# Which queues carry v, the stores and the first q and k of an attention and MLP-mixer kernel

## The chip, the cores and the metric

The kernel runs on one core of one Trainium2 chip. The metric is the time of one execution on the device in microseconds. The kernel before took 317.55 us (median of three runs, 316.34 to 318.38).

The engines are named as the profile names them: PE is TensorE, DVE is VectorE, ACT is ScalarE, POOL is GpSimd, SP is SyncE. PE, DVE, ACT and POOL compute, each its own stream of instructions in order; SP here only issues transfers. A transfer is issued from the stream of one engine. Those of SP go by the hardware queue q1, those of ACT by the hardware queue q10, those of POOL by the software queue q0. On POOL an issue shows up as an instruction of that engine.

## The reference

The inputs are q, k and v of 8 batches, 8 heads, 576 positions and 64 values per head, 8 indices of global positions, and four weight matrices. Everything is float32.

```python
scores = scale * np.matmul(q, k.transpose(0, 1, 3, 2))
mask = np.abs(pos[:, None] - pos[None, :]) <= 32
mask = mask | is_global[:, None] | is_global[None, :]
scores = np.where(mask, scores, -1000000000.0)
attn = softmax(scores)                       # exp and division by the sum
x = np.matmul(attn, v)                       # (8, 576, 512), heads side by side
h = np.maximum(x.transpose(0, 2, 1) @ w_tok1, 0.0) @ w_tok2
u = x + h.transpose(0, 2, 1)
out = u + np.maximum(u @ w_ch1, 0.0) @ w_ch2
```

It is attention inside a window of 32 positions on either side, with 8 positions that see all and are seen by all, then an MLP over the 576 positions (to 256 and back) and one over the 512 channels (to 1536 and back), each added to its input.

## The kernel before

**Tiling.** The work goes batch by batch, b = 0 to 7. The 576 positions are four tiles of 128 and a last one of 64. q and k come in as float32 into the single buffers `lq` and `lk` (positions 0 to 511, two transfers of four heads each, three smaller ones in batch 0) and `lr` (the last 64 positions of both); v comes into the single buffer `lv`, five transfers, one for each tile. `cast_qk` turns q and k to float16 (`qk`, `rn`), `cast_v` turns v into `vsh`, and `shift_v` copies a half-tile shift of it to `vod`. q and k must be transposed: for batches 0 to 2 (below `PEB` = 3) PE does it (`turn_pe`, `rest_pe`), and for batches 3 to 7 nine DMA transposes of each batch do it from SP (`turn_dma`, lines 639 and 643), after which DVE copies `raw` to `qT` and `kT` (lines 651 and 654).

**Stages of a batch.** `scores` multiplies the window's blocks, ACT takes exp into `e` (line 683), DVE masks (line 689). The rows of the global positions come in by an indirect load on POOL (`f_gather`, line 487) into `g32`, are cast (line 617) and transposed in `glob_rows`; batch 0 has its global rows out of `glob_pe` instead, so the gathered rows serve batches 1 to 7, in two groups. `values` multiplies by v and DVE normalises into `x` (lines 780 to 790). `token1` and `token2` are the MLP over positions; their sum `u` is transposed by `turn_u`, by PE for batches 0 to 2 and by DMA from SP after that (lines 843 and 853). `chan1` multiplies by the first channel weight (line 866), ACT or DVE evict with relu (lines 858 and 860), `chan2` multiplies by the second (line 895) and DVE adds `u` into one of three `osb` buffers (line 903), from which a transfer of 256 KB stores a tile of the output. The last tiles of two batches share one `osb` and go out as two transfers (line 909).

**What sets the order.** Every step is entered with `op`: the engines that may do it with their costs, a priority, what it reads and writes, and for a transfer `dma` = (time on the DMA engines, packet size, latency, packets). `behind` names steps that must have been issued before. Then `run` plans the whole kernel as the program is built. It places step after step on the engine that is free first, by priority among those that could start about then, and models the queues and their sharing of the DMA engines. For a transfer that is planned after 36 us its users are planned another 2 us later, and `late` adds to that for one step. The plan fixes only the order of each engine's stream; on the chip an engine waits until its next instruction can start. So a changed cost or queue can change the order on every engine.

**Who issues what.** SP: q, k and v of batch 0, q and k of batches 3 to 7, all DMA transposes, all stores. ACT: v of batches 3 to 7 (five issues a batch, 25 in all). POOL: the weights, which are cast on the way, the gathers, q and k of batches 1 and 2, v of batches 1 and 2. `gate` makes POOL wait for the first v tiles of batch 0 before it issues the weights and what comes behind them. After the second gather POOL has nothing to do.

Of the kernel before, what the change touches and what calls it, by code (L numbers as in the profile page):

```python
# [15 lines left out]
P = 128  # L16
# [11 lines left out]
def kernel(  # L28
# [12 lines left out]
    nc = tc.nc  # L41
# [845 lines left out]
    def chan2(b, tau, pri):  # L887
# [17 lines left out]
        if not last:  # L905
            op([("S", 0.45)], pri + 5, lambda e: nc.sync.dma_start(out=out[b, P * tau : P * tau + P, :], in_=osb), r=[("osb", o)], dma=STORE)
        else:
            for z in range(2):
                op([("S", 0.45)], pri + 5, lambda e, z=z: nc.sync.dma_start(
                    out=out[b - 1 + z, S - LAST : S, :], in_=osb[64 * z : 64 * z + 64]), r=[("osb", o)], dma=(0.39, 2048, 0.8, 64))  # L910
# [11 lines left out]
    def loads(b, n0=0):  # L922
        pl = 100.0 * b - 145 if b != 1 else -174.0
        if b == 0:
# [6 lines left out]
            return  # L931
        if b < PEB:
            if b == 1:
                pl = -173.9
            load_rest(b, pl, [("G", 0.73)], [n0] if b == 1 else ())
            for h in range(0, H, 4):
                for ti in range(2):
                    load_qk(b, ti, slice(h, h + 4), pl + 1 + h / 2 if b > 1 else pl + 0.1 + h / 100, [("G", 0.88)], [n0] if b == 1 else ())
            if b > 1:
                load_v(b, pl + 6, [("G", 0.87)])  # L940
        else:
            load_rest(b, pl, [("S", 0.65)])
# [13 lines left out]
    for b in range(B):  # L956
# [102 lines left out]
```

## Time and profile before

| | |
|---|---|
| median of the runs | 317.55 us (316.34 to 318.38, three runs) |
| the profiled execution | 317.08 us, of which the span of the records is 315.4 us |
| mean granted clock of PE | 0.984 |
| matrix multiplications of the channel MLP (lines 866 and 895) | 93.3 and 87.8 us of PE's busy time |
| bytes moved by DMA | 51.31 MB, mean 163 GB/s |
| share of the 16 DMA engines' span: q1, q0, q10 | 48.7%, 16.5%, 9.9% |

All times in the profile are from one execution, in microseconds from the start of the span. The engines' busy times overlap. A queue's share is the time of its packets against 16 engines; when several queues run at once the shares can add up to more than 1. In a timeline a line gives the start, the duration, the engine, the line of the kernel, the operation, what it writes and reads, how many such instructions are merged, and in brackets how long the engine had been idle before it and whose end released it. A name with a q at the end, such as SPq or ACTq, is the engine's sequencer, which issues transfers and handles semaphores. A list of waits gives the waiting instruction, what it waited for, then the total in us, how often, and the longest.

### The profile page before, as it was taken

The page shows a single profiled execution, that of the slowest core. Times are in us where ns is not written, and L with a number is a line of the kernel's source. Part 1 is how long each engine was busy: PE and PEld are TensorE (multiplying, and loading weights), DVE is VectorE, ACT ScalarE, POOL GpSimd, SP SyncE. Part 2 cuts the span into 40 slices and gives each one's busy share as a digit, 9 for nine tenths or more (in the row PEclk, how much of TensorE's full clock was granted, in tenths as well). Part 3 has the DMA queues.
Part 4 walks back from the last instruction along what each step waited for, and adds up shares of the span by engine and source line. Part 5 has one row for each costly group of instructions (what it writes and reads, how often), then busy time and mean ns, then how long its engine had stood idle before and what let it go on. Part 6 is the DMA issues. An engine that isn't in the chain of part 4 may idle for free.

```text
span 315.4 us, 7280 instructions
## 1 busy us (share of the span) xinstructions
PE 291.4 (92%) x2944; PEld 153.3 (49%) x2944; DVE 187.6 (59%) x413; ACT 178.7 (57%) x322; POOL 44.5 (14%) x81
## 2 busy tenths in 40 slices
PE   6968989997999898999999996799999999999993
PEld 3635645453474444444475443444465445444641
DVE  7588867569777587586675657772554257230021
ACT  4872895479996484965985693541832182305500
POOL 8588735620000000000000000000000000000000
PEclk9779999999999999799999999999999999999999
DMA  6999999999599979999999989415001401051013
GB/s 179 253 135 295 207 221 246 275 254 265 122 238 214 209 207 301 162 217 223 310 164 153 304 192 203 109 22 164 33 2 31 137 35 36 11 160 49 2 67 100
DMA packets 96452, 51.31 MB, mean 163 GB/s; under 512 B 73698, under 2 KB 89954, under 8 KB 96418
## 3 DMA queue, kind: packets, MB, share of 16 engines
q1 hardware_dynamic: 66512, 33.83, 48.7%
q0 software_dynamic: 6464, 11.11, 16.5%
q10 hardware_dynamic: 23442, 5.90, 9.9%
q8 instruction: 23, 0.38, 0.5%
q14 instruction: 11, 0.09, 0.1%
HBM read 36.11 MB, written 9.44 MB: 144 GB/s over the span
## 4 chain that ended last, share of the span: by engine, by line
PE 49%; DMA 24%; DVE 11%; ACT 10%; issue 2%; SPq 2%; ACTq 1%; POOL 0%; DVEq 0%
PE bank L895 19%; PE bank L866 16%; DMA raw<-qk 9%; DMA lq<-in_q_dram 5%; DMA g_q<-in_q_dram,idx_i 4%; PE bank L821 3%; ACT e L683 3%; PE bank L803 3%; ACT b L858 3%; DMA lk<-in_k_dram 2%; PE bank L673 2%; ACT qk L534 2%; PE bank L878 2%; DVE qT L569 1%; DMA lv<-in_v_dram 1%
## 5 line engine op out<-in xcount | busy, mean ns | idle before, releaser
L866 PE MATMUL bank<-uT,wc 128*128 128x512 f16 x384 | 93.3, 384 | 3.6 <-DVE qT L589 1.3
L895 PE MATMUL bank<-wc,b 128*128 128x512 f16 x384 | 87.8, 379 | 0.1
L858 ACT ACTIVATE b<-bank 128x512 f16<-128x512 f32 x86 | 50.9, 614 | 42.8 <-PE bank L866 36.9
L683 ACT ACTIVATE e<-bank 128x648 f16<-128x648 f32 x64 | 42.8, 730 | 35.0 <-PE bank L673 33.9
L895 PEld LDWEIGHTS <-b 128*128 128x128 f16 x384 | 36.9, 98 | 43.5 <-issue 0.4
L866 PEld LDWEIGHTS <-wc 128*128 128x128 f16 x384 | 35.3, 98 | 45.1 <-issue 6.9
L903 DVE TENSOR_TENSOR osb<-u,bank 128x512 f32<-128x512 f16 x32 | 21.7, 685 | 40.5 <-PE bank L895 40.2
L689 DVE TENSOR_TENSOR e<-e,masku 128x1296 f16<-128x1296 f16 x28 | 23.2, 830 | 17.0 <-ACT e L683 16.7
L546 ACT CAST vsh<-lv 128x512 f16<-128x512 f32 (+3 forms) x44 | 27.1, 620 | 5.2 <-DMA lv<-in_v_dram 4.1
L834 DVE TENSOR_TENSOR u<-x,bank 128x512 f16<-128x512 f16 x30 | 18.7, 682 | 13.1 <-PE bank L821 12.8
L781 DVE TENSOR_TENSOR x<-bank,rr 128x512 f16<-128x512 f32 x32 | 22.1, 691 | 1.1
L740 PE MATMUL bank<-rf,lf 128*64 128x264 f16 x144 | 15.1, 278 | 5.8 <-ACT b L858 2.0
L821 PE MATMUL bank<-a,w 128*128 128x512 f16 x80 | 19.9, 379 | 0.3 <-DVE a L809 0.2
L651 DVE COPY kT<-raw 128x512 f16<-128x512 f16 x20 | 12.0, 601 | 13.5 <-DMA raw<-qk 13.4
L803 PE MATMUL bank<-x,w 128*128 128x512 f16 x64 | 19.2, 387 | 0.5 <-DMA lq<-in_q_dram 0.4
L673 PEld LDWEIGHTS <-kT 64*128 64x128 f16 x576 | 11.6, 98 | 14.7 <-issue 13.9
L534 ACT CAST qk<-lq 128x512 f16<-128x512 f32 x26 | 15.9, 623 | 4.0 <-DMA lq<-in_q_dram 4.0
L534 ACT CAST qk<-lk 128x512 f16<-128x512 f32 x27 | 16.6, 625 | 2.6 <-DMA lk<-in_k_dram 2.6
L673 PE MATMUL bank<-qT,kT 64*128 64x72 f16 x576 | 15.9, 199 | 0.5 <-ACT e L683 0.4
L753 PEld LDWEIGHTS <-e 128*64 128x64 f16 x576 | 15.3, 111 | 0.2
L753 PE MATMUL bank<-vsh,e 128*64 128x66 f16 x320 | 15.3, 194 | 0.0
L654 DVE COPY qT<-raw 128x512 f16<-128x512 f16 x20 | 11.9, 601 | 4.8 <-DMA raw<-qk 4.8
(163 smaller groups left out, 321.2 us busy)
## 6 DMA issues: line engine op xcount, KB each, us to landing
out_dram<-osb SPq DMA_DIRECT2D x32, 256.0 KB, 2.5
lq<-in_q_dram SPq DMA_DIRECT2D x11, 512.0 KB, 6.2
lk<-in_k_dram SPq DMA_DIRECT2D x11, 512.0 KB, 7.6
lv<-in_v_dram ACTq DMA_DIRECT2D x15, 256.0 KB, 5.1
wc<-in_moe_w_ch_dram POOLq DMA_DIRECT2D x6, 512.0 KB, 12.6
lq<-in_q_dram POOLq DMA_DIRECT2D x4, 512.0 KB, 12.1
lk<-in_k_dram POOLq DMA_DIRECT2D x4, 512.0 KB, 10.1
lv<-in_v_dram ACTq DMA_DIRECT2D x10, 192.0 KB, 3.9
```

The source lines that it names most:

```text
L534: COPY[e](out=qk[:, ti, p].rearrange("q i (r d) -> q r i d", r=2), in_=(lq, lk)[ti][:, hs])
L546: COPY[e](out=vsh[i][a:z, c, :, 0:D], in_=lv[a:z, c])
L673: nc.tensor.matmul(ps_tile[keys[z]][:, u // 3, UW * (u % 3) : UW * (u % 3) + UW], lhsT=kT[r, 64 * u : 64 * u + P], rhs=qT[r, u // 2, UW * ...
L683: op([("A", 0.595)], pri + 1, lambda e, par=par: nc.scalar.activation(out=es[i][:, 2 * p + par].rearrange("p (n u) x -> p n u x", n=3), in ...
L689: op([("V", 0.85)], pri + 2, lambda e: nc.vector.tensor_mul(out=e2, in0=e2, in1=masku.unsqueeze(1).to_broadcast([P, 2, NB, UW])), r=["mask ...
L753: nc.tensor.matmul(o[:, VW * hh : VW * hh + VW], lhsT=es[i][:, h, 2 * tau + c, x : x + 64], rhs=vod[i][:, tau, h, :] if c else vsh[i][:, t ...
L781: nc.vector.tensor_tensor(out=xo, in0=pq[:, :, :, 0:D], in1=rr.unsqueeze(3).to_broadcast([P, 2, NP, D]), op=ALU.mult,)
L803: nc.tensor.matmul(ps_tile[key][:, tt], lhsT=w, rhs=x16s[i][:, ch, :], start=(ch == 0), stop=(ch == NT - 1))
L821: nc.tensor.matmul(ps_tile[key], lhsT=w2[:, ch, P * tau - sh : P * tau - sh + P], rhs=a1[:, ch, :], start=(ch == 0), stop=(ch == 1 and not ...
L858: nc.scalar.activation(out=out, in_=in_, func=AF.Relu)
L866: nc.tensor.matmul(ps_tile[key], lhsT=wc1[:, cc, P * j : P * j + P], rhs=uT[:, cc, :], start=(cc == 0), stop=(cc == 3))
L895: nc.tensor.matmul(ps_tile[key], lhsT=w, rhs=wc2[:, j, :], start=(j == 0), stop=(j == NJ - 1))
```

## The change

- **v**: the loads of batches 3 to 7 go from ACT's queue to POOL's. Batch 2 was there already, so v of batches 2 to 7 is on POOL now (30 transfers), planned at 0.87 us each. v of batch 0 stays on SP and of batch 1 on POOL.
- **Stores**: the stores of whole tiles of batches 0 to 6 (28 transfers) go from SP to POOL, planned at 0.8 us each. Batch 7's four stores and the eight of the last tiles stay on SP.
- **q and k**: batches 1 and 2 go from POOL to SP (12 transfers). All q and k is on SP then, planned at 0.55 us an issue instead of 0.5. Those of batch 1 no longer stand behind the gate; they have a priority right after batch 0's v.
- **Order**: the second channel weight's first part is to be issued behind the last part of the first channel weight (`n1`), no longer behind batch 1's loads. The first gather, that of q for the first group, has `late` = 2.3, so the plan has its cast on DVE that much later.

```diff
@@ chan2
         if not last:
-            op([("S", 0.45)], pri + 5, lambda e: nc.sync.dma_start(out=out[b, P * tau : P * tau + P, :], in_=osb), r=[("osb", o)], dma=STORE)
+            op([("G", 0.8) if b < B - 1 else ("S", 0.45)], pri + 5, lambda e: ENG[e].dma_start(out=out[b, P * tau : P * tau + P, :], in_=osb), r=[("osb", o)], dma=STORE)
...
@@ loads
-        if b < PEB:
-            if b == 1:
-                pl = -173.9
-            load_rest(b, pl, [("G", 0.73)], [n0] if b == 1 else ())
-            for h in range(0, H, 4):
-                for ti in range(2):
-                    load_qk(b, ti, slice(h, h + 4), pl + 1 + h / 2 if b > 1 else pl + 0.1 + h / 100, [("G", 0.88)], [n0] if b == 1 else ())
-            if b > 1:
-                load_v(b, pl + 6, [("G", 0.87)])
-        else:
-            load_rest(b, pl, [("S", 0.65)])
-            for h in range(0, H, 4):
-                for ti in range(2):
-                    load_qk(b, ti, slice(h, h + 4), pl + 1 + h / 2, [("S", 0.5)])
-            load_v(b, pl + 6, [("A", 0.6)])
+        load_rest(b, pl, [("S", 0.65)])
+        for h in range(0, H, 4):
+            for ti in range(2):
+                load_qk(b, ti, slice(h, h + 4), pl + 1 + h / 2, [("S", 0.55)])
+        if b > 1:
+            load_v(b, pl + 6, [("G", 0.87)])
@@ the loop over batches
-                op([("G", 2.7)], (-115 if ti == 0 else -174.2) if b == 0 else 70, f_gather(b, ti), r=["idx"], w=[("g32", b, ti)], dma=(0.1, 256, 1.7, 256),
+                op([("G", 2.7)], (-115 if ti == 0 else -174.2) if b == 0 else 70, f_gather(b, ti), r=["idx"], w=[("g32", b, ti)], dma=(0.1, 256, 1.7, 256), late=0.0 if b or ti else 2.3,
...
-            loads(1, n0)
-            op([("G", 0.77)], -40, f_wc2(0), w=[("wc2", 0)], dma=(2.6, 4096, 2.0, 512), behind=[len(ops) - 1])
+            loads(1)
+            op([("G", 0.77)], -40, f_wc2(0), w=[("wc2", 0)], dma=(2.6, 4096, 2.0, 512), behind=[n1])
```

More of the change, by code (lines that the diff above doesn't have):

```diff
@@ L905, in chan2 @@
         if not last:
-            op([("S", 0.45)], pri + 5, lambda e: nc.sync.dma_start(out=out[b, P * tau : P * tau + P, :], in_=osb), r=[("osb", o)], dma=STORE)
+            op([("G", 0.8) if b < B - 1 else ("S", 0.45)], pri + 5, lambda e: ENG[e].dma_start(out=out[b, P * tau : P * tau + P, :], in_=osb), r=[("osb", o)], dma=STORE)
         else:
             for z in range(2):
-                op([("S", 0.45)], pri + 5, lambda e, z=z: nc.sync.dma_start(
+                op([("S", 0.45)], pri + 5, lambda e, z=z: ENG[e].dma_start(
                     out=out[b - 1 + z, S - LAST : S, :], in_=osb[64 * z : 64 * z + 64]), r=[("osb", o)], dma=(0.39, 2048, 0.8, 64))
```

## The prediction

> **What bounds the kernel now.** I read the page's head first, then busy time by stretch, then what TensorE (PE) waited for in each stretch that is not full, and last the engines named there.
>
> ```profile
> span 315.4 us, 7280 instructions
> PE 291.4 (92%) x2944; PEld 153.3 (49%) x2944; DVE 187.6 (59%) x413; ACT 178.7 (57%) x322; POOL 44.5 (14%) x81
> ```
> ```profile
> 0.00:20.00 20.00, 14.21 (x174) 9.73 (x175) 14.75 (x62) 12.72 (x23) 14.23 (x41) 0.87 0.90 199
> 20.00:60.00 40.00, 36.82 (x491) 20.94 (x489) 30.14 (x69) 25.66 (x49) 27.24 (x37) 0.98 1.08 241
> 60.00:140.00 80.00, 74.80 (x753) 38.91 (x751) 58.21 (x119) 58.84 (x107) 2.99 (x3) 0.98 1.11 219
> 140.00:180.00 40.00, 39.92 (x392) 20.49 (x391) 27.36 (x53) 26.77 (x50) 0.00 (x0) 1.00 1.16 232
> 180.00:200.00 20.00, 15.20 (x234) 8.22 (x232) 11.90 (x27) 12.96 (x24) 0.00 (x0) 1.00 0.96 208
> 200.00:300.00 100.00, 100.00 (x874) 50.50 (x868) 41.82 (x81) 41.72 (x72) 0.00 (x0) 1.00 0.20 54
> ```
>
> Columns of the second: stretch and length, busy time of PE, weight loads, VectorE (DVE), ScalarE (ACT) and GpSimd (POOL), granted clock, DMA share, GB/s. PE is the bound: 291.4 of 315.4 us, and full from 200 to 300, when the loads are over. Only its idle time, 24.0 us, can be won. By stretch that is 20 less 14.21 = 5.8, then 3.2, 5.2, 0.1 and 4.8: 19.1 us before 200 us. The rest lies at the end, where this change leaves SyncE (SP) and its stores as they are. Up to 200 us the DMA share is around 1 or above, so the loads are hardly ahead of their users. What PE waited for, in four windows (up to 55, 55 to 80, 105 to 130, 189 to 200 us):
>
> ```profile
> PE bank L666 <- DVE qT L569: 2.4, 2, 2.1
> ```
> ```profile
> PE bank L866 <- DVE qT L589: 1.3, 1, 1.3
> ```
> ```profile
> PE bank L740 <- ACT b L858: 2.0, 2, 1.3
> PE bank L866 <- DVE osb L903: 1.2, 1, 1.2
> ```
> ```profile
> PE bank L740 <- DVE x L781: 1.9, 1, 1.9
> PE bank L740 <- DVE rf L726: 1.4, 1, 1.4
> PE bank L720 <- DVE eg L692: 1.1, 1, 1.1
> ```
>
> These waits (total, times, longest) are what the change can reach: 2.4 + 1.3 + 2.0 + 1.2 + 4.4 = 11.3 us.
>
> **Part by part. v off ScalarE.** Batches 3 to 7 issue five v loads each from ACT's stream, 25 in all; they go to POOL. The timeline of ACT at two of PE's holes:
>
> ```profile
> 121.98 2.06 ACTq L523 DMA_DIRECT2D lv<-in_v_dram  x1
> 124.08 0.62 ACT L531 CAST rn<-lr 128x512 f16<-128x512 f32 x1 [3.65 <-issue]
> ```
> ```profile
> 188.48 5.79 ACTq L523 DMA_DIRECT2D lv<-in_v_dram  x3
> 194.32 0.60 ACT L858 ACTIVATE b<-bank 128x512 f16<-128x512 f32 x1 [5.44 <-DMA lv<-in_v_dram]
> ```
> ```profile
> L523 ACTq DMA_DIRECT2D lv<-in_v_dram x25: 337/391/2059, 78.7 to 197.8; - x25
> ```
> ```profile
> L523 POOL DMA_DIRECT2D lv<-in_v_dram x10: 789/882/901, 28.6 to 57.2; - x10
> ```
>
> An issue normally holds ACT's queue 0.39 us, but one took 2.06, and three together 5.79. In the second case ACT computed nothing for 5.44 us, with the exps and relu evictions that feed PE queued behind the issues. The 1.1 and 1.4 us waits follow it, and the 2.0 us wait for `b` follows the first case. Gain if all of it goes: 1.1 + 1.4 + 2.0 = 4.5 us; I take 4.0, since something else is late a little after. PE's idling there also costs clock:
>
> ```profile
> 125.00:130.00 5.00, 3.54 (x36) 1.68 (x36) 2.94 (x8) 4.94 (x10) 0.00 (x0) 0.75 1.46 195
> ```
>
> 3.54 us at 0.75 are 2.65 us at full clock, so 0.9 us more. On POOL the 25 issues cost 0.88 each, 22 us of an engine without any work after 66 us (POOL is 2.99 busy in 60 to 140, then 0.00).
>
> **Stores off SyncE.** 28 stores (four of each of batches 0 to 6) leave SP. SP is a serial queue, and in the last hole it stands on the path:
>
> ```profile
> 185.10 0.54 SPq L906 DMA_DIRECT2D out_dram<-osb  x1
> 185.69 4.26 SPq L643 DMA_TRANSPOSE raw<-qk  x3
> 190.04 0.53 SPq L906 DMA_DIRECT2D out_dram<-osb  x1
> 190.66 1.28 SPq L643 DMA_TRANSPOSE raw<-qk  x1
> ```
>
> It issues without a pause, transposes of 1.28 to 1.4 us with stores of 0.54 between. DVE's copies of `raw` wait for these transposes and stand ahead of the `x` that PE waited 1.9 us for. Two stores here (1.07 us) and the two just before them come off. I take 1.0 of the 1.9. Likewise before PE's 1.2 us hole DVE waited for `raw`:
>
> ```profile
> 108.57 0.61 DVE L651 COPY kT<-raw 128x512 f16<-128x512 f16 x1 [1.70 <-DMA raw<-qk]
> ```
>
> I take 0.5 there. This row also gives an exchange rate: 1.70 us of DVE waiting became 1.17 us of PE idle (the 1.2 above, rounded), 0.7 to 1. On POOL 28 stores cost 28 x 0.88 = 25 us, beside other work. A late store delays the DVE add that wants its `osb` buffer again, and behind that add stand DVE's relu evictions, mask products and normalisations. Landing times, issue to landing, in the last column:
>
> ```profile
> out_dram<-osb SPq DMA_DIRECT2D x32, 256.0 KB, 2.5
> ...
> lv<-in_v_dram POOLq DMA_DIRECT2D x6, 256.0 KB, 11.1
> ```
> ```profile
> 275.35 7.77 PE bank L895 x36
> ```
>
> No store on POOL is in the trace; its landing lies between SP's 2.5 and the 11.1 us of a 256 KB load on POOL. 36 matmuls make three output tiles, so one of three buffers is wanted again every 7.77 us; less 0.69 for the add, 7.1 us are there. 0.88 + 2.5 = 3.4 us fits, 0.88 + 11.1 = 12.0 does not. I take the low end, cost nothing: the 11.1 was met while half-megabyte loads of batch 2 stood ahead in POOL's queue, and these leave it.
>
> **q and k of batches 1 and 2 onto SyncE.** Twelve issues (two `lr`, four `lq`/`lk` for each batch). SP had this room:
>
> ```profile
> 5.91 8.72 SPq L523 DMA_DIRECT2D lv<-in_v_dram  x5
> 56.05 0.60 SPq L514 DMA_DIRECT2D lr<-in_q_dram  x1
> ```
>
> At 0.6 us each they are 7.2 us in 41 us of idle SP (14.6 to 56), no cost there; behind them stand only batch 3's loads. POOL loses the same twelve, so weights, v and the second gather start earlier. PE's 1.3 us hole came from that second gather, which DVE awaited here:
>
> ```profile
> 69.41 0.23 DVE L617 CAST g_q<-g_q 128x128 f16<-128x128 f32 x1 [1.80 <-DMA g_q<-in_q_dram,idx_i]
> ```
>
> I take 1.0 of the 1.3. Batch 1's loads now run beside weights instead of ahead of them in one queue; with PE idle 3.2 us in all from 20 to 60 I put this at nothing, from 2 us better (the largest part of those 3.2) to 2 us worse (the same again).
>
> **Gathered rows later.** The first `g_q` cast goes behind other DVE work:
>
> ```profile
> 15.48 0.30 DVE L617 CAST g_q<-g_q 128x128 f16<-128x128 f32 x1 [1.70 <-DMA g_q<-in_q_dram,idx_i]
> ```
>
> The `qT` copies that end PE's 2.1 us wait stand behind this cast in DVE's order. The stall of 1.70 bounds the gain; I take 1.3, as v's own landing is next.
>
> **What it costs.** POOL's queue (q0) crowds out SP's (q1) when both are full, as in 56 to 62 us:
>
> ```profile
> q0 software_dynamic: 469, 1.61, 100.6%
> q1 hardware_dynamic: 101, 0.03, 3.1%
> ```
>
> q0 moved 1.61 MB and q1 0.03 (packets, MB, share of the 16 DMA engines), with SP's loads for batch 3 already issued. Five v loads issued in a row are 5 x 0.88 = 4.4 us of this per batch, against SP's transposes of batches 3 to 7. The bounds are nothing (issues spread by the casts that free `lv`) and 5 x 4.4 x 0.7 = 15.4 us. I take two new holes of the size of the 1.2 us one, 2.4 us, since PE sat idle 0.1 us in 140 to 180 with the same DMA share and so has other work to fill in.
>
> The Trainium skill, "DMA: Bandwidth & Descriptors", section on queues, rings and completion order, says that a DMA engine takes turns among the queues that have work, a whole packet at a time. The row of q0 and q1 agrees in kind and is more one-sided than taking turns suggests; even turns would make this cost smaller than its upper bound.
>
> The build lays out every engine's order anew from the changed costs. PE's work is the same and the order stays one of filling, so I price that at nothing, within the same 2 us either way as the loads of batch 1.
>
> Sum: 4.0 + 0.9 + 1.0 + 0.5 + 1.0 + 1.3 = 8.7 off, 2.4 on, 6.3 net. The profiled execution took 317.08 us (span 315.4 and 1.7 around it), 0.5 below the median of the runs shown, 317.55. 317.08 - 6.3 = 310.8 us.
>
> **The rivals.** *Transposes starve* (slower): v's bursts on q0 hold back the `raw` transposes, DVE stands at a `raw` copy with everything behind it. For it: the 56 to 62 us rows, and that DVE's wait for `raw` already opened a hole. Against it: PE's backlog in 140 to 180, and that stores and v's small pieces stop competing inside q1 and q10. With the full 15.4 us against 8.7 of gains: 323.8 us. It decides from 8.7 / (5 x 0.7) = 2.5 us of extra DVE waiting per batch; 25%.
>
> *Nothing to measure*: ACT no longer stands at its issues, but the loads land when they did, because the DMA engines are full (shares of 0.96 to 1.16 from 20 to 200 us), and PE finds the next late thing. Only the gather gains stay, 1.0 + 1.3, against 2.4: 317.2 us, with 3 us either way; 18%.
>
> *Stores late* (slower): if a store takes 12.0 us instead of 7.1, DVE stands 4.9 us once in each of seven batches, at 0.7 that is 24 us: 317.1 - 8.7 + 24 = 332 us. The Trainium skill, "SBUF — State Buffer", section "SBUF: two separate sides", warns of a way there: DVE copies in the two-port modes lock GpSimd out of a shared port, so it cannot write its descriptors; it advises against POOL's queue beside such copies. The ten v issues on POOL spread only from 789 to 901 ns with DVE at work beside them, so I see at most 0.1 us of that here; 5%.
>
> **How the numbers follow.** My forecast 52%; its own range is 304 to 314, from 11.3 + 0.9 us gained with nothing paid (304.9, and a little for loads that come earlier) to half the gains. A measurement of this kernel tells about 1% from no change, 314.4 to 320.7 around 317.55. Faster: the 52% with about a twentieth of it lost to the middle, and 3% from the edge of *nothing to measure*: 0.53. Within 1%: 0.18 less that edge and plus that twentieth, with a tenth of the starving: 0.20. Slower: the rest, 0.27. The range reaches down to 304 and up to 324, where the starving rival's full price ends; beyond lie the late stores and about a tenth of the rest.
>
> **What would show it.** Right: no ACT gap over 2 us behind an L523 in 100 to 200; PE at least 18 busy in 180 to 200 (or in the 20 us in which the last loads land); SP's transposes without stores between; DVE without the 1.70 wait near 15 us; stores on POOL landing in 2.5 to 5 us. Wrong: DVE's total wait for `raw` at L651 well above what the waits show now:
>
> ```profile
> DVE kT L651 <- DMA raw<-qk: 13.4, 9, 2.7
> ```
>
> DVE waiting for a store's landing at L903; PE idle above 24.0 us in all. The forecast fails if POOL's in-order queue, where v loads and stores now wait for one another's ACT casts and DVE adds, lets either run late.

## The result and the profile after

The changed kernel took 330.41 us (median of four runs, 329.9 to 333.62) against 317.97 us before (four runs, 316.34 to 318.62). The ratio is 1.040, with a 95% interval of 1.033 to 1.047: the change costs 12.4 us where the prediction had a gain of 6.3. The profiled execution is the longest of those runs, 333.62 us with a span of 331.8; it shows where the time goes, but 3.2 us more of it than the median has. Medians are over all executions here and below, while ratios and their intervals leave out those in a slower state.

The head of the page of the changed kernel, and busy time by stretch with the same columns as before (PE, weight loads, DVE, ACT, POOL, granted clock, DMA share, GB/s):

```profile
span 331.8 us, 7342 instructions
...
PE 297.0 (90%) x2950; PEld 155.9 (47%) x2950; DVE 187.4 (56%) x410; ACT 180.1 (54%) x325; POOL 74.7 (23%) x122
```
```profile
0.00:20.00 20.00, 16.24 (x214) 10.99 (x214) 15.09 (x65) 14.54 (x27) 14.72 (x41) 1.00 0.97 219
20.00:60.00 40.00, 29.51 (x331) 16.22 (x332) 25.45 (x55) 21.43 (x43) 20.64 (x28) 0.83 1.15 245
60.00:140.00 80.00, 77.14 (x851) 41.49 (x849) 56.53 (x115) 62.42 (x116) 21.28 (x27) 1.00 0.99 216
140.00:180.00 40.00, 34.06 (x334) 16.84 (x332) 25.75 (x54) 25.21 (x47) 9.01 (x12) 1.00 1.00 212
180.00:200.00 20.00, 13.54 (x82) 6.78 (x80) 6.85 (x11) 3.75 (x7) 1.14 (x2) 0.83 1.00 161
200.00:300.00 100.00, 100.00 (x990) 50.28 (x989) 53.63 (x106) 43.78 (x75) 7.36 (x13) 1.00 0.24 63
```

The span grew by 16.4 us: PE's idle time from 24.0 to 34.8 us (331.8 less 297.0), 10.8 more, and its busy time by 5.6. The busy time is the same work at a lower clock: 297.0 us at the mean granted clock of 0.967 are 287.2 us at full clock, before 291.4 at 0.984 are 286.7. So the whole loss is idle time and a lower clock, 0.83 in 20 to 60 and in 180 to 200, the two stretches with the largest share of idle time. That idling lowers the clock is an inference: before, PE idled 4.8 of the 20 us from 180 to 200 at a clock of 1.00. By stretch (length less PE's busy time):

| PE idle, us | 0 to 60 | 60 to 140 | 140 to 200 | 200 to 300 |
|---|---|---|---|---|
| before | 9.0 | 5.2 | 4.9 | 0 |
| changed | 14.3 | 2.9 | 12.4 | 0 |

There are two losses, 5.3 us at the start and 7.5 us late, and between them a gain of 2.3. What PE waited for in the two stretches that lost (0 to 60, then 140 to 200 us; total, times, longest):

```profile
PE bank L866 <- DVE b L860: 5.6, 1, 5.6
PE bank L720 <- DVE eg L692: 2.4, 1, 2.4
PE bank L566 <- ACT qk L534: 1.5, 1, 1.5
```
```profile
PE bank L895 <- DVE u L834: 8.3, 2, 6.5
PE bank L895 <- DVE osb L903: 1.8, 1, 1.8
```

A wait names only the last link. The timeline of DVE, PE and SP in the first loss tells what stood behind it:

```profile
21.37 0.42 DVE L546 CAST vsh<-lv 96x512 f16<-96x512 f32 x1 [2.47 <-DMA lv<-in_v_dram]
...
33.30 1.26 DVE L534 CAST qk<-lk 128x512 f16<-128x512 f32 x1 [2.63 <-DMA lk<-in_k_dram]
...
34.59 0.69 DVE L809 TENSOR_SCALAR a<-bank 128x512 f16<-128x512 f32 x1
...
41.44 8.09 SPq L514 DMA_DIRECT2D lr<-in_q_dram  x1
...
48.47 0.76 DVE L534 CAST qk<-lq 128x512 f16<-128x512 f32 x2 [6.85 <-DMA lq<-in_q_dram]
49.15 0.68 DVE L860 TENSOR_SCALAR b<-bank 128x512 f16<-128x512 f32 x1
...
49.88 1.86 PE L866 MATMUL bank<-uT,wc 128*128 128x512 f16 x4 [5.57 <-DVE b L860]
```

The largest hole, 5.57 us of PE, is the fifth and sixth line from the top read together with the last: DVE's relu eviction `b`, which PE needs, needs nothing that is late. It stands behind the cast of batch 2's `lq` in DVE's order, and that cast waited 6.85 us for a load that now goes by SP's queue. The load is not later than it was. In the kernel before the same `lq` was first cast here:

```profile
56.71 0.62 ACT L534 CAST qk<-lq 128x512 f16<-128x512 f32 x1 [0.68 <-DMA lq<-in_q_dram]
```

That is 8.2 us after the cast at 48.47. What is new is that the planned order wants this `lq` from 41.6 us on, ahead of `b`. The cast of batch 1's `lk` does the same on a smaller scale at 33.30, with the eviction `a` behind it. At 21.37 it is the last tile of v of batch 0; SP issues the last two tiles behind batch 1's `lr` loads now. SP itself was held at a single issue for 8.09 us.

Late, the timeline of POOL, SP, DVE, PE and ACT:

```profile
168.55 4.64 POOL L523 DMA_DIRECT2D lv<-in_v_dram  x5 [9.72 <-ACT vsh L546]
...
176.89 7.64 SPq L639 DMA_TRANSPOSE rawr<-rn  x1
...
181.59 0.61 DVE L651 COPY kT<-raw 128x512 f16<-128x512 f16 x1 [7.32 <-DMA raw<-qk]
...
184.64 8.69 SPq L643 DMA_TRANSPOSE raw<-qk  x4
...
186.15 0.59 DVE L654 COPY qT<-raw 128x512 f16<-128x512 f16 x1 [3.21 <-DMA raw<-qk]
...
188.05 2.47 DVE L834 TENSOR_TENSOR u<-x,bank 128x512 f16<-128x512 f16 x4
...
188.79 11.42 PE L895 MATMUL bank<-wc,b 128*128 128x512 f16 x40 [6.46 <-DVE u L834]
189.09 1.14 ACT L534 CAST qk<-lq 128x512 f16<-128x512 f32 x2 [10.84 <-DMA lq<-in_q_dram]
```

Five v loads leave POOL within 4.64 us. After them the transposes are late: SP's queue stands 7.64 us at the one of `rn`, and DVE stands 7.32 us at a copy of `raw`, then 3.21 us at the next; the sum `u` is four instructions behind the first, and PE stands 6.46 us for `u`. ACT waits 10.84 us for q of batch 7, which is on SP's queue too. How the queues shared the DMA engines, in 30 to 36 us and in 174 to 180 us (packets, MB, share of the 16 engines):

```profile
q0 software_dynamic: 907, 0.91, 88.9%
q1 hardware_dynamic: 907, 0.29, 31.2%
```
```profile
q0 software_dynamic: 183, 0.60, 85.5%
q1 hardware_dynamic: 582, 0.14, 16.8%
```

In the first, each queue sent 907 packets: one for one, but POOL's are 1.0 KB and SP's 0.32 KB, so POOL's queue moved three times the bytes. In the second, a packet of v on POOL's queue is 0.60 MB / 183 = 3.3 KB and takes 0.855 x 6 x 16 / 183 = 0.45 us of an engine; SP's queue got 0.14 MB through in 6 us. The engines weren't full all that time: in slices of 0.15 us their share goes up and down between under one tenth and over nine tenths. Why SP's queue got so little through is not shown.

The stores, from the groups by line and from the page's last part, did what was hoped:

```profile
L906 POOL DMA_DIRECT2D out_dram<-osb x28: 542/542/857, 81.1 to 302.4; - x28
```
```profile
out_dram<-osb POOLq DMA_DIRECT2D x28, 256.0 KB, 3.7
lv<-in_v_dram POOLq DMA_DIRECT2D x21, 256.0 KB, 9.1
```

A store's issue takes 0.54 us on POOL and lands after 3.7 us in the median; a v load lands after 9.1.

### The profile page after: what moved, and what is told of

Its sections match the earlier page's. It is cut to its first block, busy times and chain, and to the rows that moved or that the text cites. A ratio compares the mean times of both kernels' runs of the same rounds, so it can differ in the third digit from the quotient of the medians.

```text
span 331.8 us, 7342 instructions
## 1 busy us (share of the span) xinstructions
PE 297.0 (90%) x2950; PEld 155.9 (47%) x2950; DVE 187.4 (56%) x410; ACT 180.1 (54%) x325; POOL 74.7 (23%) x122
## 4 chain that ended last, share of the span: by engine, by line
PE 51%; DMA 26%; DVE 7%; ACT 5%; issue 5%; SPq 2%; POOL 1%; ACTq 0%; POOLq 0%; DVEq 0%
PE bank L895 23%; PE bank L866 16%; DMA wc<-in_moe_w_ch_dram 11%; DMA raw<-qk 8%; DMA lv<-in_v_dram 5%; PE bank L821 3%; PE bank L673 2%; PE bank L803 2%; PE bank L753 2%; PE bank L740 2%; DMA w1l<-in_moe_w_tok_dram 2%; PE bank L878 2%; ACT e L683 1%; DMA lk<-in_k_dram 1%; ACT vsh L546 1%
## 5 line engine op out<-in xcount | busy, mean ns | idle before, releaser
L866 PE MATMUL bank<-uT,wc 128*128 128x512 f16 x384 | 94.8, 385 | 6.9 <-DVE b L860 5.6
L895 PE MATMUL bank<-wc,b 128*128 128x512 f16 x384 | 89.6, 387 | 10.0 <-DVE u L834 8.3
L858 ACT ACTIVATE b<-bank 128x512 f16<-128x512 f32 x90 | 53.6, 613 | 40.0 <-PE bank L866 39.9
L895 PEld LDWEIGHTS <-b 128*128 128x128 f16 x384 | 37.7, 100 | 55.6 <-issue 14.2
L866 PEld LDWEIGHTS <-wc 128*128 128x128 f16 x384 | 35.4, 98 | 48.7 <-issue 10.2
L906 POOL DMA_DIRECT2D out_dram<-osb x28 | 16.2, 580 | 153.6 <-DVE osb L903 149.3
L523 POOL DMA_DIRECT2D lv<-in_v_dram x35 | 31.7, 913 | 60.9 <-ACT vsh L546 46.4
L534 ACT CAST qk<-lq 128x512 f16<-128x512 f32 x29 | 17.4, 631 | 25.3 <-DMA lq<-in_q_dram 25.2
L546 ACT CAST vsh<-lv 128x512 f16<-128x512 f32 (+3 forms) x40 | 23.4, 617 | 1.9 <-DMA lv<-in_v_dram 1.4
L803 PE MATMUL bank<-x,w 128*128 128x512 f16 x64 | 20.1, 401 | 0.0
L673 PEld LDWEIGHTS <-kT 64*128 64x128 f16 x576 | 11.4, 97 | 15.5 <-issue 15.0
L651 DVE COPY kT<-raw 128x512 f16<-128x512 f16 x20 | 12.4, 622 | 10.0 <-DMA raw<-qk 9.8
L673 PE MATMUL bank<-qT,kT 64*128 64x72 f16 x576 | 15.7, 198 | 1.5 <-ACT e L683 1.4
L554 DVE COPY vod<-vsh 64x2112 f16<-64x2112 f16 (+1 forms) x18 | 12.3, 684 | 6.4 <-ACT vsh L546 6.0
## 6 DMA issues: line engine op xcount, KB each, us to landing
wc<-in_moe_w_ch_dram POOLq DMA_DIRECT2D x6, 512.0 KB, 13.1
```

Of the source, the lines that this page charges most:

```text
L523: ENG[e].dma_start(out=lv[r0:r1, c], in_=v[b, :, j0 : j0 + (r1 - r0), :].rearrange("h p d -> p h d"))
L534: COPY[e](out=qk[:, ti, p].rearrange("q i (r d) -> q r i d", r=2), in_=(lq, lk)[ti][:, hs])
L546: COPY[e](out=vsh[i][a:z, c, :, 0:D], in_=lv[a:z, c])
L673: nc.tensor.matmul(ps_tile[keys[z]][:, u // 3, UW * (u % 3) : UW * (u % 3) + UW], lhsT=kT[r, 64 * u : 64 * u + P], rhs=qT[r, u // 2, UW * ...
L803: nc.tensor.matmul(ps_tile[key][:, tt], lhsT=w, rhs=x16s[i][:, ch, :], start=(ch == 0), stop=(ch == NT - 1))
L858: nc.scalar.activation(out=out, in_=in_, func=AF.Relu)
```

## The experiments

The change moves three kinds of transfers to other queues, and through the plan it moves nearly everything in time as well. Two theories: *queues* (A in the forecasts; A1 for v beside the transposes, A2 for q and k beside the weights), by which the transfers themselves are slower or slow others where they are now, and *order* (B), by which the newly planned streams are worse. After the first eight runs came a third (C): *mismatch*, by which a stream reads data sooner than its queue now brings it, so that queue and order do harm together. Two kinds of kernel tell these apart. "Old order" and "new order" keep every engine's planned instructions of one kernel and change only the engine whose queue issues a transfer; a "replanned" kernel gives the planner the other queue, as the change does. The runs of one letter shared a chip with runs of the kernel before (c1 with the b runs; medians of before 316.56 to 317.57 us), and ratios are against those.

| run | v of batches 3 to 7 | stores | q, k of batches 1, 2 | order | median, us | ratio (95%) |
|---|---|---|---|---|---|---|
| the change | POOL | POOL | SP | new | 330.41 | 1.040 (1.033 to 1.047) |
| a1 | POOL | POOL | SP | old | 328.2 | 1.034 (1.026 to 1.042) |
| a2 | ACT | SP | POOL | new | 341.89 | 1.077 (1.068 to 1.085) |
| a3 | ACT | POOL | SP | new | 341.23 | 1.072 (1.062 to 1.082) |
| a4 | POOL | POOL | POOL | new | 330.88 | 1.032 (1.020 to 1.044) |
| b2 | POOL | SP | POOL | old | 323.7 | 1.021 (1.016 to 1.026) |
| b3 | ACT | SP | SP | old | 317.07 | 0.999 (0.995 to 1.004) |
| b4 | ACT | POOL | POOL | old | 313.86 | 0.991 (0.988 to 0.994) |
| e4 | ACT | POOL | SP | old | 318.37 | 1.006 (1.000 to 1.011) |
| c1 | ACT | SP | POOL | replanned, gather late | 317.93 | 1.002 (0.999 to 1.006) |
| d1 | ACT | POOL | SP | replanned | 325.85 | 1.028 (1.021 to 1.034) |
| d2 | ACT | POOL | POOL | replanned | 318.85 | 1.003 (0.998 to 1.007) |
| d3 | ACT | SP | SP | replanned | 337.26 | 1.066 (1.059 to 1.072) |
| d4 | POOL | POOL | SP, users later | replanned | 333.41 | 1.041 (1.033 to 1.049) |

PE's idle time in the profiled execution of those whose stretches are used below, from rows like those above (length less busy):

| PE idle, us | 0 to 60 | 60 to 140 | 140 to 200 |
|---|---|---|---|
| a1, old order, all new queues | 12.0 | 3.0 | 5.6 |
| a2, new order, old queues | 12.0 | 7.6 | 12.2 |
| b2, old order, v alone on POOL | 9.5 | 6.8 | 5.4 |
| d1, v back on ACT | 14.7 | 3.3 | 4.7 |
| d3, only q and k moved | 14.6 | 3.3 | 11.5 |
| d4, q and k planned later | 9.6 | 10.7 | 6.4 |
| e1, little v | 16.1 | 0.9 | 2.2 |
| e2, little q and k | 7.4 | 7.1 | 7.9 |
| e3, before with little of both | 8.7 | 0.1 | 3.6 |

Each row is one execution. Two kernels were profiled twice (b4 again as f1, d2 again as f2), and a stretch differed by up to 3.2 us between the two (4.7 and 7.9 us in 60 to 140 for d2 and f2), so smaller differences in this table show nothing.

### Queues against order

The whole change of queues in the old order:

```diff
@@ load_qk, load_rest
-            ENG[e].dma_start(
+            (nc.sync if b in (1, 2) else ENG[e]).dma_start(
@@ load_v
-                ENG[e].dma_start(
+                (nc.gpsimd if b >= PEB else ENG[e]).dma_start(
@@ chan2
-            ... lambda e: nc.sync.dma_start(out=out[b, ...
+            ... lambda e: (nc.gpsimd if b < B - 1 else nc.sync).dma_start(out=out[b, ...
```

> The order of every compute engine is that of the kernel before; only the queues are the changed ones (v of batches 3 to 7 and the stores of batches 0 to 6 issued by POOL, q and k of batches 1 and 2 by SP, at the places the old plan gave them). Theory A, the queues: what costs is that POOL's queue and SP's share the DMA engines, so batch 1's and 2's q and k land late beside the weights and the transposes crawl beside v; then this run is as slow as the change, 326 to 334 us. Theory B, the order: what costs is the new plan (casts of batch 1 put ahead of batch 0's evictions on DVE and ACT); then it stays near the kernel before, 314 to 321 us.

328.2 us. The queues alone, with the old order on every compute engine, cost most of what the change costs. That speaks against *order* by itself. In this run PE also idles 4.6 us after 200 us, behind a transpose that the chain of waits shows (start, length):

```profile
192.86 11.28 DMA raw<-qk
```

One DMA transpose was under way for 11.28 us; POOL issued five v loads from 189.21 to 193.68 us beside it.

The reverse is the changed kernel's order with the same three lines turned back:

> The changed kernel's order on every engine, with the old queues (v of batches 3 to 7 on ACT, stores on SP, q and k of batches 1 and 2 on POOL). Theory A, the queues: 314 to 321 us, PE idle before 200 us back near 19 us. Theory B, the order: it stays slow, 326 to 334 us.

341.89 us, 11.5 us slower than the change. The new order is far worse on the old queues, slower than either theory had it, which speaks against *queues* by itself. What PE waited for in 140 to 200 us of this run:

```profile
PE bank L821 <- ACT a L812: 5.6, 1, 5.6
PE bank L866 <- ACT b L858: 5.1, 1, 5.1
```

Both waits are for ACT: v's issues are in ACT's stream again, one of them 2.41 us long at 179.44 us, in an order that was planned without them. Only v turned back, and only q and k turned back, in the new order:

> The changed kernel with its own order; only v of batches 3 to 7 is issued by ACT again. PE fell 7.6 us behind between 140 and 200 us in the changed kernel. Theory A puts this on v's packets beside the transposes, so most of it comes back here: 321 to 326 us, and DVE's 7.3 us wait for a transpose near 174 us is gone. Theory B, the order: within 3 us of 330. A third, the stores: also within 3 us of 330.

> The changed kernel with its own order; only q and k of batches 1 and 2 are issued by POOL again, in one queue with the weights. PE was 10.9 us behind at 60 us in the changed kernel. Theory A puts this on q and k sharing the engines with the weights packet by packet, so it comes back here: 318 to 323 us, and DVE's 6.9 us wait for lq near 42 us is gone. Theory B, the order: within 3 us of 330, as the casts still stand ahead of the evictions.

With v on ACT 341.23 us, which neither forecast had; it is as bad as a2, so v accounts for nearly all that a2 lost. With q and k on POOL 330.88, no change that shows. Yet DVE's wait for `lq` in the first 60 us is gone there, as *queues* had forecast; PE idles 13.4 us in that stretch all the same, 3.7 of them for a fill of `kT` that stands behind loads in POOL's stream. The new order is worse on the queues that it wasn't planned for, so these runs can't price a move; the ones in the old order and the replanned ones have to.

### One move at a time, old order

Each with one of the three lines of a1:

> The kernel before with its own order on every engine; only v of batches 3 to 7 is issued by POOL instead of ACT. With all three queue changes the old order took 328.2 us against 317.3, with one hole of 4.6 us after 200 us behind a transpose that took 11.3 us beside v's packets. Theory A1, v's packets beside the transposes: 4 to 7 us slower than before, 321 to 325 us, and a raw transpose over 8 us long among those that run while v is under way. Rival, v off ACT only helps (no ACT stall of 5.4 us near 190 us): 310 to 316 us.

> The kernel before with its own order; only q and k of batches 1 and 2 are issued by SP instead of POOL. Theory A2, q and k sharing the engines with the weights: 5 to 7 us slower, 322 to 325 us, with PE's work left at 60 us 5 or more above the 240.3 us of before. Rival, only the order is at fault in the first 60 us: within 2 us of 317.

> The kernel before with its own order; only the stores of batches 0 to 6 are issued by POOL instead of SP. Stores on POOL landed in a median of 2.4 us with the old order, so theories A1 and A2 expect no loss: 314 to 318 us, a gain if SP's transposes come earlier. Rival, the stores are part of the loss: 320 us or more.

v alone costs 7.1 us (323.7 against 316.56), q and k alone nothing, and the stores alone gain 2.7. With v alone moved, DVE's waits in 60 to 200 us were:

```profile
DVE kT L651 <- DMA raw<-qk: 10.9, 8, 3.4
...
DVE osb L903 <- DMA out_dram<-osb: 5.4, 1, 5.4
```

A store that is still on SP's queue is late here, by 5.4 us at 82.22 us, and PE waited 2.5 us for the add behind it; the transposes are not the only ones on SP's queue that v holds up. From 69 to 76 us, when that store was on its way, SP's queue moved 0.97 MB beside 0.92 MB of v; in the kernel before, with the same order, it moved 1.83 MB. The forecast's sign, a transpose over 8 us long, tells nothing: the longest landing of a `raw` was 8.1 us here and 8.4 before.

> The kernel before in its own order, with q and k of batches 1 and 2 on SP and the stores on POOL, v left on ACT. Alone these gave +0.0 and -0.9%. If all that the three queue changes lost together (328.2 us) hangs on v: 313 to 316 us. If q, k and stores hurt together: 319 us or more.

318.37 us lies between the two forecasts. Beside 313.86 for the stores alone, the stores' gain is gone when q and k are on SP as well. Against e4, v on POOL in a1 adds 9.8 us (328.2 against 318.37, on two chips).

The fourth part of the change, the gather's cast planned later:

```diff
@@ the loop over batches (before)
-                op([("G", 2.7)], ..., f_gather(b, ti), ..., dma=(0.1, 256, 1.7, 256),
+                op([("G", 2.7)], ..., f_gather(b, ti), ..., dma=(0.1, 256, 1.7, 256), late=0.0 if b or ti else 2.3,
```

> The kernel before, planned anew with the one number late = 2.3 for the first gather and nothing else. If the 1.7 us stall of DVE near 15 us passes on to PE: 315 to 316.5 us. If v's landing holds the batch then: 317 to 318 us. What it moves further on is the measure of what a mere change of order does.

317.93 us, nothing. The stall of DVE near 15 us is gone and PE's idle time in 0 to 20 us is 5.1 us instead of 5.8; PE finds the next late thing.

### Replanned kernels

The change with v back on ACT (in `loads`):

```diff
-            load_v(b, pl + 6, [("G", 0.87)])
+            load_v(b, pl + 6, [("A", 0.6) if b >= PEB else ("G", 0.87)])
```

> The changed kernel planned anew with one thing undone: v of batches 3 to 7 on ACT, so that the order fits the queue again. Theory A1, v on POOL is the largest part (7 us in the old order): 319 to 324 us, with PE's work left still near 251 us at 60 us but no further loss between 140 and 200 us. Rival, the loss lies in q and k and the order they bring: 327 us or more.

325.85 us, between the two forecasts and 4.6 below the change (on two chips): that much is v's move when each version has its own plan. The late loss goes (4.7 us idle in 140 to 200, as before), and the early one stays: 14.7 us in 0 to 60, with DVE waiting 6.1 us for `lq` and PE 4.8 us for `b` behind it, the same pair as in the change.

With the stores back on SP too, so that q and k are nearly all that is left:

```diff
-            op([("G", 0.8) if b < B - 1 else ("S", 0.45)], pri + 5, ...
+            op([("S", 0.45)], pri + 5, ...
```

> The changed kernel planned anew with v of batches 3 to 7 on ACT and the stores on SP, so what is left of the change is q and k of batches 1 and 2 on SP (and the late first gather). In the old order q and k on SP cost nothing (317.1 us). Theory C, the new plan trusts q and k to land earlier than they do and puts their casts ahead of batch 0's evictions: 322 to 328 us, with PE's work left at 60 us near 250 us. Rival, q and k on SP are harmless: 316 to 319 us.

337.26 us, worse than the whole change and than the forecast of *mismatch*. q and k on SP, which cost nothing in the old order (b3), cost 20 us in the plan that is made for them. With the stores on POOL (d1) it is 11.4 us less, so the stores' move seems a gain there as well, though each of the two has its own plan. Why 140 to 200 us is bad here, with v where it was, was not followed up; PE's waits there are for ACT's exp (9.3 us), and ACT waits 10.8 us for transposes of `raw` and 7.3 us for v. So a late loss of this size can come without v on POOL.

Then the early loss, by its own repair: the users of the q and k of batches 1 and 2 are planned later, about as much as the loads came late.

```diff
-        load_rest(b, pl, [("S", 0.65)])
+        load_rest(b, pl, [("S", 0.65)], late={1: 6.0, 2: 10.0}.get(b, 0.0))
...
-                load_qk(b, ti, slice(h, h + 4), pl + 1 + h / 2, [("S", 0.55)])
+                load_qk(b, ti, slice(h, h + 4), pl + 1 + h / 2, [("S", 0.55)], late={1: 6.0, 2: 10.0}.get(b, 0.0))
```

> The changed kernel on its own queues, planned anew with q and k of batch 1 taken to land 6 us later and those of batch 2 10 us later than the plan thought, which moves their casts behind batch 0's evictions. Theory C: the loss of the first 60 us shrinks by half or more, PE's work left at 60 us 246 us or less, in all 322 to 327 us. Rival, what is lost there is lost to the shared engines whatever the order: within 3 us of 330.

333.41 us, no gain, where *mismatch* had 322 to 327; and yet its mechanism holds. In the change PE waited 5.6 us for `b` and DVE 6.8 us for `lq` in the first 60 us; here neither is left among the four longest waits of its engine, and the idle time there is 9.6 us, near the 9.0 of the kernel before. It comes back in the next stretch, 60 to 140 us:

```profile
PE bank L866 <- DVE osb L903: 6.3, 2, 4.5
```
```profile
DVE osb L903 <- DMA out_dram<-osb: 5.5, 1, 5.5
```

Here a store on POOL is late and the add stands in front of a relu eviction, as a cast did before. *Mismatch* explains the early loss; repairing that one place does not repair the kernel.

### Less traffic, same order

If the losses come from bytes that are late and not from the order as such, they must go when the bytes go, with nothing else changed. In the changed kernel, first v is cut to one head of eight, then q and k to one of four (in `load_v`, `load_qk` and `load_rest`); the rest of each buffer keeps old values, so these kernels are for timing only:

```diff
+                n = 1 if b >= PEB else H
-                    out=lv[r0:r1, c], in_=v[b, :, j0 : j0 + (r1 - r0), :]...
+                    out=lv[r0:r1, c, 0:n], in_=v[b, 0:n, j0 : j0 + (r1 - r0), :]...
```

> The changed kernel with the same instructions in the same order on every engine, but each v transfer of batches 3 to 7 brings one head of eight (the other heads keep what lay in the buffer), so v's traffic on POOL's queue is an eighth. The changed kernel idles PE 12.4 us between 140 and 200 us. If v's packets beside q, k and the transposes make that loss: 6 us or less there, and 320 to 325 us. If the order makes it: 10 us or more there, within 3 us of 330.

```diff
-                in_=(q, k)[ti][b, hs, 0 : S - LAST, :]...
+                in_=(q, k)[ti][b, slice(hs.start, hs.start + 1) if b in (1, 2) else hs, 0 : S - LAST, :]...
...
-                    ... in_=ten[b, :, S - LAST : S, :]...
+                    ... in_=ten[b, 0 : 1 if b in (1, 2) else H, S - LAST : S, :]...
```

> The changed kernel, same instructions and order, but the q and k transfers of batches 1 and 2 bring one head of four (of the last 64 positions one head of eight). The changed kernel idles PE 14.3 us in the first 60 us, the kernel before 9.0. Theory C, casts in front of the evictions wait for q and k that land late: 10 us or less there, and 321 to 326 us in all. If the order loses it even with the data in time: 13 us or more, within 3 us of 330.

319.45 us (1.006, 1.001 to 1.010) and 318.69 us (1.000, 0.995 to 1.005). Busy time by stretch, of the run with little v and then of the run with little q and k (0 to 60 and 140 to 200 us):

```profile
0.00:60.00 60.00, 43.94 (x522) 26.42 (x522) 39.66 (x118) 34.55 (x66) 34.46 (x68) 0.86 1.08 233
...
140.00:200.00 60.00, 57.79 (x610) 29.78 (x610) 42.31 (x86) 35.99 (x66) 7.62 (x13) 1.00 0.86 179
```
```profile
0.00:60.00 60.00, 52.56 (x675) 32.06 (x676) 46.86 (x134) 42.89 (x82) 38.70 (x72) 0.97 1.05 224
...
140.00:200.00 60.00, 52.15 (x496) 25.83 (x495) 34.51 (x70) 34.22 (x62) 9.65 (x13) 0.94 0.91 184
```

PE's busy time is the first number after the comma. Little v: the late loss is gone (57.79 of 60), the early one isn't (43.94). Little q and k: the early loss is gone (52.56), and 4.5 us of the late one went with it. Each cut repairs its own stretch, though with little q and k 60 to 140 us idles 7.1 us where the change had 2.9. The order is the same in both, so neither loss comes of the order alone. But less traffic may help any kernel, so the kernel before got both cuts:

> The control for the other two: the kernel before, same instructions and order, with both cuts (v of batches 3 to 7 to one head of eight, q and k of batches 1 and 2 to one of four). If less traffic alone is worth much in any kernel: 308 us or less. If the loads of the kernel before are hidden but for ACT's blocked issues: 311 to 315 us.

307.95 us (0.974, 0.969 to 0.980), 9.6 us less than the 317.57 on its chip: by the forecast, less traffic is worth much in any kernel. So the total times of e1 and e2 prove little, but the stretches do. Little v takes the late idle time from 12.4 to 2.2 us, and both cuts together take it from 4.9 to 3.6 in the kernel before; little q and k take the early one from 14.3 to 7.4, and there it goes from 9.0 to 8.7. What the kernel before gains lies in 60 to 140 us (5.2 to 0.1). The two cuts in the changed kernel are worth 11.0 and 11.7 us; if they add up, which wasn't run, that is 13.1 more than in the kernel before, near the 12.4 us that the change costs.

The traces of all runs together tell which transfer on SP's queue v holds up. For each of batches 3 to 7 one DMA transpose takes `rn` to `rawr` (line 639 of the kernel before). In the six runs with all of this v on POOL (the change, a1, a4, b2, d4, e2) the longest landing that the profile has of the five was 9.6 to 15.7 us after the issue; with little v there (e1) it was 7.1, and 6.7 to 9.5 with v on ACT. The longest time that one such issue held SP's queue was 5.5 to 10.2 us in five of the six (2.8 in b2), and at most 4.3 in all other runs. The 40 transposes of `raw` show nothing of it in their median, 4.2 to 4.7 us in the six and 4.2 before.

### A version faster than both

The stores alone, in the old order, took 313.86 us; planned anew with that queue they didn't gain:

```diff
-            op([("S", 0.45)], pri + 5, lambda e: nc.sync.dma_start(...
+            op([("G", 0.8) if b < B - 1 else ("S", 0.45)], pri + 5, lambda e: ENG[e].dma_start(...
```

> The kernel before planned anew with one part of the change alone: the stores of batches 0 to 6 on POOL. In the old order this gave 313.9 against 316.6 us. If the gain is SP's free time: 312 to 315 us, faster than both kernels. If a new plan costs as much as it gives: 316 to 319 us.

318.85 us. The two had run on different chips, so both were run again on one:

> The kernel before with its own order on every engine, the whole-tile stores of batches 0 to 6 issued from GpSimd; the same kernel as the earlier run of the stores alone (0.991). If that gain is real: a ratio of 0.986 to 0.996, below 317 us by 1.3 to 4.5 us. If it was the luck of one call: 0.997 to 1.003.

> The stores alone on GpSimd, with the order that the build plans for them; the same kernel as the earlier replanned run (1.0025), here beside the one with the old order on one chip. If the new plan gives the gain away: 0.998 to 1.007, and slower than its neighbour by 2 to 5 us. If the two runs differed only by their calls: the same ratio as its neighbour within 0.004.

314.94 us (0.994, 0.991 to 0.998) and 320.65 us (1.004, 0.998 to 1.010), beside 317.25. The stores on POOL in the old order are faster than the kernel before by 0.6 to 0.9%, and so than both kernels; the gain is small but came twice. The new plan gives it away. In the timeline of the second replanned run:

```profile
77.96 0.69 DVE L903 TENSOR_TENSOR osb<-u,bank 128x512 f32<-128x512 f16 x1 [4.94 <-DMA out_dram<-osb]
78.70 1.86 PE L866 MATMUL bank<-uT,wc 128*128 128x512 f16 x4 [5.16 <-DVE osb L903]
```

An `osb` buffer is wanted again before its store has landed, and 5.16 us of PE go there. In the run with the old order DVE's waits for a store sum to 1.2 us. But this stall does not come in every execution: in the profile of the same kernel as d2, 314.96 us, these waits are 0.3 us. How much of the median it explains is open.

## Why the prediction was wrong

Two terms failed. The crowding of SP's queue by v was put at 2.4 us, where v alone made the kernel 7.1 us slower in the old order; and q and k on SP together with the new order were put at nothing, where PE idled 5.3 us more in the first 60 us.

**What bounds the kernel: right.** PE is full where it has work, and the result is idle time before 200 us plus clock. The end, from 200 us, is as full as before.

**v off ScalarE: the gain is not shown, and the price was wrong.** No ACT instruction stands behind an issue of L523 any more, and from 60 to 140 us PE's idle time fell from 5.2 to 2.9 us. That fall can't be put down to v: with v back on ACT it is 3.3 us (d1), with v alone on POOL 6.8 (b2), and two executions of one kernel differ by up to 3.2. The prediction had a 4.0 us gain here, and 0.9 of clock, against a crowding of SP's queue of 2.4, the value chosen between 0 and 15.4. That step failed: 140 to 200 us went from 4.9 to 12.4 us idle (7.5 more) and the clock to 0.83 at its end; v alone costs 7.1 us in the old order, all gains included, and 4.6 between two planned versions. The reason given for the low end, that PE had other work to fill in, was read from a stretch in which transposes were not yet held up: 0.1 us idle at a DMA share of 1.16 proves cover only as long as DVE's copies aren't late by more than the work queued on PE. One wait of 7.32 us at a `raw` copy is more than that. Two of the chosen signs came: PE idled more than 24.0 us in all (34.8), and was 13.54 us busy in 180 to 200, not 18. A third, DVE's total wait at L651 above 13.4 us, did not show:

```profile
DVE kT L651 <- DMA raw<-qk: 9.8, 4, 7.3
```

The total fell from 13.4 to 9.8; the longest rose from 2.7 to 7.3. Many short waits were covered, one long one was not. The sign should have been the longest wait, and ACT's wait for q (10.84 us), which the prediction didn't price at all: it counted only the transposes as victims on SP's queue. In b2 one victim is a store.

**The rival *Transposes starve* had this part right in kind**: DVE stands at a `raw` copy with everything behind it. v alone in the old order is 7.1 us slower with its gains in it. If the 4.9 forecast for those (4.0 and 0.9) came in whole, which b2 doesn't show, the price is 12 us, an estimate, where the rival had 15.4 and the forecast 2.4. It was to decide from 2.5 us of extra DVE waiting in each of five batches; in the trace it came at one place above all, with 7.32 us at once. The rival's 323.8 us fell short of the result because the early loss was in none of the cases. The 332 us of *Stores late* lie nearest to the result, by luck: the stores were not what cost the time.

**q and k onto SyncE, with the new order: the other step that failed.** "Nothing, from 2 us better to 2 us worse" was 5.3 us more idle in 0 to 60 us, with the clock at 0.83 in 20 to 60. In 29.51 busy us that is 5.0 us at full clock, where 36.82 at 0.98 had lost 0.7. SP did have the room, though the twelve issues held it about 22 us and not 7.2. Beside weights its queue sent packet for packet (907 and 907), with packets a third as large. But batch 2's `lq` came sooner than in the kernel before, not later (cast at 48.47 us, before at 56.71). What failed is the price of the new order, which was put "at nothing, within the same 2 us": it asks for that `lq` from 41.6 us on, with a relu eviction behind it. b3 shows that the move costs nothing in the old order. e2 shows that with early data the new order idles PE no more in these 60 us than the old one (7.4 us, and 8.7 in e3). The two together cost the most, 20 us in d3. The prediction had no term for the two together.

**Stores off SyncE: right in sign, and the value taken was near.** 0.54 us an issue (0.88 was taken), landing 3.7 us (3.4 with the issue was taken). Alone in the old order the stores gain 2.3 and 2.7 us by the medians on two chips, where 1.5 were forecast. *Stores late* has not come as a rule, one stall of 4.9 us in each of seven batches, but single stalls of about that size did: 5.5 us in d4 and 4.94 in f2. The Trainium skill, "SBUF — State Buffer", section "SBUF: two separate sides", advises against POOL's queue beside DVE's two-port copies; here POOL's store issues stayed at 0.54 us in the median (857 ns the longest) and of the kernels with full traffic the one with only the stores moved, in the old order, is the fastest, so this case shows no such loss for the stores; no run was made to test it.

**The gathers: right about the stall, wrong about its worth.** DVE's 1.70 us wait near 15 us is gone, but the next late thing is v's last tile at 21.37 us, and c1 shows the same: 1.002. "As v's own landing is next" stood in the prediction, and 1.3 us were counted all the same.

**Taking turns.** The Trainium skill, "DMA: Bandwidth & Descriptors", section on queues, rings and completion order, has a DMA engine take whole packets in turn from the queues that have work. The prediction concluded that even turns would make the crowding smaller than its upper bound. The trace agrees with the turns from 30 to 42 us (907 and 907, 735 and 734) and not with the conclusion: even turns in packets are uneven in bytes when one queue's packets are three times as large.

**Open.** How much of the late loss is the transposes and how much q of batches 6 and 7 was not separated: e1 takes v away from both. What PE waited for late is mostly `u`, 8.3 us, behind the copies of `raw`; what ACT's waits for q (8.72 us at 150.66 and 10.84 at 189.09) cost PE isn't known. Nor is it known why d3's plan does so badly late with v on ACT. e1, e2 and d4 settle the two places in the changed kernel; they don't say which order would suit the new queues.

## What to carry to other kernels

Where the order of the engines is planned, moving a transfer to another queue and planning anew is two changes at once: run the new queue in the old order first (b3, b4), then with its plan (d2, d3), and keep the old order if that is faster. Price a load on a shared queue by the packets that run beside it, and by the longest wait of an in-order engine that reads it, with what stands behind that wait; a total of waits, or a full engine in the stretch, hides it. A step that is blocked on its engine is only worth moving if the transfer doesn't then hold up those that the engines wait for next.

## What the runs showed of the hardware that was not expected

From 30 to 42 us of the changed kernel the two queues with work shared the DMA engines one packet for one packet: 907 to 907 in 30 to 36 us and 735 to 734 in 36 to 42 us. It isn't so everywhere: 353 (POOL) to 1083 (SP) in 56 to 62 us, and 183 to 582 in 174 to 180 us, beside transposes.

v on POOL's queue held up SP's queue without taking more of the engines than v on ACT's. From 70 to 315 us q10 moved 5.90 MB before in 12.7% of 16 engines over these 245 us, 498 us of packet time, 11.8 KB per us. In b2, where v alone moved, q0 moved 5.91 MB in 10.8%, 423 us, 14.0 KB per us, in packets of 3.2 KB instead of 0.25. Single stretches are worse: in 174 to 180 us of the changed kernel it was 0.60 MB in 82 us, 7.3 KB per us.

POOL issues a store in 0.54 us and a v load in 0.89 (medians of 28 and 35 in the changed kernel), though 21 of these loads move the same 256 KB as a store.
